# Moving the upper partitions' eighth rows of the last w_o piece to the lower 64 partitions

## The chip, the cores and the metric

The kernel runs on one core of one Trainium2 chip. The metric is the device time of one execution in microseconds (us), as the median of several runs. A profiled execution gives a trace beside it; its times count from the span's start.

## What is computed

One decode step (one row x of 576 numbers) through two branches, mixed by a gate:

```python
g = sigmoid((x * gate_w).sum())
a = attention(x @ wq, last 4096 keys and values of 16 kv heads, 32 query heads) @ wo
b = gelu(x @ w1 + b1) @ w2 + b2
return g * a + (1 - g) * b
```

w_o is 4096 x 576 and w2 is 4608 x 576, all inputs in bf16. Nothing is reused between outputs: each weight and each cached key or value is read once, 53.62 MB in all.

## The kernel before

All large loads are issued by SyncE (SP), one after the other, in the order in which the code stands: keys, wq, w1 and values, then w_o (line 617), then w2 (line 627), and at last the store of the result (line 702). Each lands in SBUF in a tile of a pool: `w_pool` has three buffers (tag "w", for wq, w1 and w_o), `kv_pool` six (tag "kv", for keys, values and w2). The whole kernel is scheduled by hand, so each engine runs its instructions in the order written.

**The loads of w_o.** Head groups of eight heads (OJ = 8, NOG = 4): in group o, partition p holds the rows o·1024 + 8p + j, j = 0 to 7, of w_o, next to each other. Line 617 loads two groups with one transfer, 128 partitions x 2 x 9,216 bytes (2304 KB); `wo_t[0]` holds groups 0 and 1, `wo_t[1]` groups 2 and 3. This text calls the two transfers wo0 and wo1.

**The loads of w2.** Four groups of 9 rows per partition. Groups 0, 1 and 2 (w2_0, w2_1, w2_2 here) are one transfer of 1296 KB each; group 3 comes in three pieces of 864, 288 and 144 KB (w2_3a, b, c).

**Completion semaphores of the transfers.** The program gives SP's transfers eight semaphores in turn (DMAHW0 to DMAHW7). Before a transfer is issued, SP waits until the transfer that had the same semaphore before, the eighth before it, has landed. SP handles its instructions strictly in order, so while one transfer waits, those behind it aren't issued. Before the change the last ones stand so in SP's list (row number, line, shape in elements, what SP waits for):

```
39 L102 v_t      64x8192     [waits DMAHW2]
40 L617 wo_t (wo0)   128x2x4608  [waits DMAHW3]
41 L617 wo_t (wo1)   128x2x4608  [waits DMAHW4]
42 L627 w2_t (w2_0)  128x5184    [waits DMAHW5, PE]
43 L627 w2_t (w2_1)  128x5184    [waits DMAHW6, PE]
44 L627 w2_t (w2_2)  128x5184    [waits DMAHW7, PE]
45 L627 w2_t (w2_3a) 128x3456    [waits DMAHW0, PE]
46 L627 w2_t (w2_3b) 128x1152    [waits DMAHW1]
47 L627 w2_t (w2_3c) 128x576     [waits DMAHW2]
48 L702 out      4x144       [waits DMAHW3, DVE]
```

**The end of the kernel.** After the last attention values, DVE scales the head outputs (`ot`, line 631), eight small matmuls lay them out by partition (`ow_ps`, line 637), and DVE picks each partition's own head by a mask (`ow_m`, line 639) and a sum (`ow`, line 647): `ow[p, j, o]` is the factor for row j of partition p in group o. Then, at line 669, `blocks` of four columns are multiplied on TensorE into the accumulator `part`: first w_o's eight blocks, each with two matmuls of 288 columns per row, 64 matmuls; then the blocks of w2_0, w2_1, w2_2 with 18 matmuls each. DVE adds the bias and scales (`part_s`, line 677). At line 688 eight matmuls collect part_s and 36 matmuls multiply w2's last group into `y_ps`; DVE copies `y` (line 701) and SP stores it (line 702).

Of the kernel before, what the change touches and what calls it, by code (L numbers as in the profile page):

```python
# [8 lines left out]
FP32 = mybir.dt.float32  # L9
BF16 = mybir.dt.bfloat16  # L10
ACT = mybir.ActivationFunctionType
ALU = mybir.AluOpType
# [4 lines left out]
def kernel(  # L17
# [15 lines left out]
    nc = tc.nc  # L33

    P = 128
    D = 576
    Hq, Hkv, Dh = 32, 16, 128
# [41 lines left out]
    const = ctx.enter_context(tc.tile_pool(name="const", bufs=1))  # L79
# [15 lines left out]
    OJ = 8  # L95
    NOG = Hq // OJ
    wo_view = A_wo.rearrange("(o p j) n -> p o (j n)", p=P, j=OJ)
# [13 lines left out]
    def load_v(m):  # L111
        return load_kv(A_v_cache, m, "v_t")

    WMAX = 36 * 256

    def load_flat(src, lo, n, name):
        t = w_pool.tile([P, WMAX], BF16, name=name, tag="w")
        nc.sync.dma_start(out=t[:, 0:n], in_=src[:, lo : lo + n])
        return t
# [17 lines left out]
    for i in range(2):  # L137
# [16 lines left out]
        out=row_f[:], in_=ident_f[:, 0 : 32 * (NQ - 1) + 1 : 32], axis=AX.X, op=ALU.add  # L154
# [4 lines left out]
        out=dup[:].rearrange("k (i e) -> k i e", e=2),  # L159
        in_=ident[0 : P // 2, 0 : P // 2].rearrange("k (i e) -> k i e", e=1).to_broadcast(  # L160
            [P // 2, P // 2, 2]
        ),
    )
    par = const.tile([P, 2], FP32, name="par")
    for o in range(2):
        nc.vector.tensor_reduce(
            out=par[:, o : o + 1],
            in_=ident_f[:].rearrange("p (i o) -> p o i", o=2)[:, o, :],
# [7 lines left out]
        out=turn[:].rearrange("p j (h q) -> p j h q", h=OJ),  # L176
        in_=ident[:].rearrange("p (o q j) -> p j o q", o=1, j=OJ).to_broadcast(
            [P, OJ, OJ, P // OJ]
        ),
# [4 lines left out]
        out=m_r[:], in_=ident_f[:].rearrange("p (s r) -> p r s", r=R), axis=AX.X, op=ALU.add  # L184
# [5 lines left out]
        out=row_e[:], in_=ident_f[:].rearrange("p (a e q) -> p e a q", e=2, q=2), axis=AX.XY,  # L190
# [3 lines left out]
        out=row_e[:], in0=row_e[:], scalar1=-MASK, scalar2=MASK, op0=ALU.mult, op1=ALU.add  # L194
    )
    mask = const.tile([P, BC * P], BF16, name="mask")
    for e in range(2):
        nc.vector.tensor_copy(
            out=mask[:, e::2], in_=row_e[:, e : e + 1].to_broadcast([P, BC * P // 2])
# [4 lines left out]
        out=m_c[:], in_=ident_f[:].rearrange("p (t c r) -> p c t r", c=BC, r=R), axis=AX.XY,  # L204
        op=ALU.add,
    )
    m_hl = const.tile([P, OJ], FP32, name="m_hl")
    nc.vector.tensor_reduce(
        out=m_hl[:], in_=ident_f[:].rearrange("p (h q) -> p h q", h=OJ), axis=AX.X, op=ALU.add
# [10 lines left out]
    for dst, src in ((sel, ident), (sel_f, ident_f)):  # L220
        nc.vector.tensor_copy(
            out=dst[:].rearrange("p l (o h) -> p l o h", o=2),
            in_=src[:].rearrange("p (h l x) -> p l x h", h=2, l=2)[:, :, 0:2, :],
# [149 lines left out]
    for dst, src, s in (  # L373
# [10 lines left out]
        out=junk[:], in0=x_row[:], in1=gw_row[:], scale=1.0, scalar=0.0,  # L384
        op0=ALU.mult, op1=ALU.add, accum_out=s0[:],
# [10 lines left out]
        out=omg[:], in0=g_t[:], scalar1=-1.0, scalar2=1.0, op0=ALU.mult, op1=ALU.add  # L396
# [7 lines left out]
    for b in range(NM * NQ):  # L404
        m, t = b // NQ, b % NQ
# [22 lines left out]
    for m in range(HB // 2):  # L428
        lo = R * (NGR - 1) + RP * m
        nc.vector.tensor_copy(  # L430
            out=qz[:, m :: HB // 2, lo : lo + RP],
            in_=qT[:, :, m, :].rearrange("p i b -> p b i"),
# [114 lines left out]
    for h in range(NU):  # L547
# [4 lines left out]
        if h == 1:  # L552

            for o in range(2):
                nc.sync.dma_start(
                    out=b1_r[o : o + 32 * (NQ - 1) + 1 : 32],
                    in_=B_b1.rearrange("(o t k n) -> o t k n", o=2, t=NQ, k=2)[o],
# [56 lines left out]
    wo_t = []  # L614
    for i in range(NOG // 2):
        t = w_pool.tile([P, WMAX], BF16, name="wo_t", tag="w")
        nc.sync.dma_start(  # L617
            out=t[:, 0 : 2 * OJ * D].rearrange("p (o n) -> p o n", o=2),
            in_=wo_view[:, 2 * i : 2 * i + 2, :],
        )  # L620
        wo_t.append(t)
    w2_t = []
    for g in range(NG):
        t = kv_pool.tile([P, NCK * Dh], BF16, name="w2_t", tag="kv")
# [7 lines left out]
        out=ot[:], in0=o_sb[:], scalar=g_t[:, 0:1], in1=r_sums[:], op0=ALU.mult, op1=ALU.mult  # L632
    )

    ow_ps = ps_m.tile([P, OJ, Hq], FP32, name="ow_ps", tag="m")
    for j in range(OJ):
# [3 lines left out]
        out=ow_m[:],  # L640
        in0=ow_ps[:].rearrange("p j (o h) -> p (j o) h", h=OJ),
        in1=m_hl[:].rearrange("p (o h) -> p o h", o=1).to_broadcast([P, OJ * NOG, OJ]),
        op=ALU.mult,
    )
    ow = const.tile([P, OJ, NOG], BF16, name="ow")
    with nc.allow_low_precision("one of the eight summands is not zero"):
        nc.vector.tensor_reduce(  # L647
            out=ow[:].rearrange("p j o -> p (j o)"), in_=ow_m[:], axis=AX.X, op=ALU.add
        )


    part = part_box[0]
    y_ps = ps_s.tile([P, DQ], FP32, name="y_ps", tag="s")
    nc.vector.memset(y_ps[:], 0.0)
    blocks = [
        [(ow[:, i, o : o + 1], wo_t[o // 2], (o % 2) * OJ + i) for i in range(j, j + NQ)]
        for o in range(NOG)
        for j in range(0, OJ, NQ)
    ]
    for g in range(NG - 1):  # L660
        for j in range(0, RJ, NQ):
            blocks.append(
                [(gt[:, i, g : g + 1], w2_t[g], i) for i in range(j, min(j + NQ, RJ))]
            )
    last = {t: max(n for n, four in enumerate(blocks) if t < len(four)) for t in range(NQ)}
    for n, four in enumerate(blocks):
# [11 lines left out]
        out=part_s[:], in0=b2_r[:].rearrange("p (k n) -> p k n", k=2), scalar=omg[:, 0:1],  # L678
        in1=part[:, :, 0:DB], op0=ALU.mult, op1=ALU.add,
# [15 lines left out]
    for j in range(RJ):  # L695
# [7 lines left out]
        out=out.rearrange("a b (t n) -> (a b t) n", t=NQ), in_=y[0 : 32 * (NQ - 1) + 1 : 32, :]  # L703
# [31 lines left out]
```

## Time and profile before

| what | value |
|---|---|
| median of 3 runs | 135.0 us (134.98 to 135.0) |
| the profiled execution's own time | 136.33 us |
| span in its trace, first to last instruction | 134.3 us |
| read from HBM | 53.62 MB, 399 GB/s over the span |
| SP's DMA queue | 94.5% of the 16 DMA engines' span |
| TensorE matmul busy | 90.8 us (68%) |
| VectorE busy | 60.2 us (45%) |
| ScalarE busy | 48.6 us (36%) |
| mean granted TensorE clock | 0.853 |

How to read it: the span is the time that the trace covers; the execution's own time has some 2 us around it, and this execution took 1.3 us more than the median of the runs. "SPq" is SyncE's sequencer, which issues transfers. A line of the timeline gives start, duration, engine, source line, operation, tile written <- tiles read, shape and count, and in brackets the idle time before it and what ended it. The profile writes `w_t` for w1 and w2 and `wo_t` for w_o.

### The profile page before, as it was taken

The page shows a single profiled execution, that of the slowest core. Times are in us where ns is not written, and L with a number is a line of the kernel's source. Part 1 is how long each engine was busy: PE and PEld are TensorE (multiplying, and loading weights), DVE is VectorE, ACT ScalarE, POOL GpSimd, SP SyncE. Part 2 cuts the span into 40 slices and gives each one's busy share as a digit, 9 for nine tenths or more (in the row PEclk, how much of TensorE's full clock was granted, in tenths as well). Part 3 has the DMA queues.
Part 4 walks back from the last instruction along what each step waited for, and adds up shares of the span by engine and source line. Part 5 has one row for each costly group of instructions (what it writes and reads, how often), then busy time and mean ns, then how long its engine had stood idle before and what let it go on. Part 6 is the DMA issues. An engine that isn't in the chain of part 4 may idle for free.

```text
span 134.3 us, 2686 instructions
## 1 busy us (share of the span) xinstructions
PE 90.8 (68%) x1127; PEld 58.1 (43%) x1127; DVE 60.2 (45%) x165; ACT 48.6 (36%) x91; POOL 5.2 (4%) x11
## 2 busy tenths in 40 slices
PE   0007985298296899397898769969969365585370
PEld 0007941265264665254565447636644141342140
DVE  4934642135127665135486544476665544400020
ACT  3003660058136787136558411557751200000000
POOL 8700000000000000000000000000000000000000
PEclk9999999959959999959999995589999965558655
DMA  3999999999999999999999999999999999999930
GB/s 78 435 431 412 406 440 444 424 448 417 426 424 429 429 449 419 412 434 424 432 420 420 434 444 420 439 424 429 434 424 429 403 436 423 422 440 423 408 128 0
DMA packets 4809, 53.79 MB, mean 400 GB/s; under 512 B 819, under 2 KB 958, under 8 KB 1342
## 3 DMA queue, kind: packets, MB, share of 16 engines
q1 hardware_dynamic: 4792, 53.62, 94.5%
q8 instruction: 9, 0.15, 0.4%
q14 instruction: 2, 0.02, 0.0%
q10 hardware_dynamic: 6, 0.00, 0.0%
HBM read 53.62 MB, written 0.00 MB: 399 GB/s over the span
## 4 chain that ended last, share of the span: by engine, by line
DMA 74%; PE 15%; DVE 6%; SPq 1%; issue 1%; DVEq 0%
DMA w_t<-in_B_w_dram 48%; DMA v_t<-in_A_v_cache_dram 17%; DMA wq_t<-in_A_wq_dram 9%; PE tp L233 6%; PE acc L340 2%; DVE kT L242 2%; PE hT L479 2%; PE s_ps L264 2%; PE y_ps L688 1%; PE part L669 1%; SPq L102 1%; DVE a_s L356 1%; DVE ez L318 1%; DVE part_s L677 1%; DVE h_r L470 1%
## 5 line engine op out<-in xcount | busy, mean ns | idle before, releaser
L244 ACT CAST kT<-tp 128x512 bf16<-128x512 f32 x80 | 44.1, 587 | 42.6 <-PE tp L233 42.3
L242 DVE CAST kT<-tp 128x512 bf16<-128x512 f32 x48 | 33.0, 690 | 36.9 <-PE tp L233 32.6
L233 PE MATMUL tp<-ident,k_t 128*128 128x128 bf16 x512 | 46.3, 242 | 4.5 <-DMA k_t<-in_A_k_cache_dram 2.9
L233 PEld LDWEIGHTS <-k_t 128*128 128x128 bf16 x512 | 35.9, 109 | 17.8 <-issue 17.1
L340 PE MATMUL acc<-v_t,ez 128*32 128x512 bf16 x128 | 13.1, 453 | 2.4 <-DVE a_s L356 2.1
L264 PE MATMUL s_ps<-kT,qz 128*32 128x512 bf16 x128 | 13.7, 423 | 0.3 <-DVE qz L430 0.3
L669 PE MATMUL part<-w_t,gt 128*1 128x288 bf16 x54 | 4.0, 384 | 4.3 <-DMA w_t<-in_B_w_dram 4.3
L452 PE MATMUL h_ps<-w_t,x 128*32 128x288 bf16 x72 | 3.1, 310 | 4.8 <-DMA w_t<-in_B_w_dram 4.8
L677 DVE SCALAR_TENSOR_TENSOR part_s<-b_r,omg,part 128x576 f32<-128x576 bf16 x1 | 0.8, 812 | 12.2 <-PE part L669 12.2
L371 PE MATMUL x_ps<-x,dup 64*128 64x9 bf16 x1 | 0.2, 163 | 8.9 <-DMA x<-in_A_x_dram 8.9
L340 PEld LDWEIGHTS <-ez 128*32 128x32 bf16 x128 | 3.7, 102 | 5.7 <-issue 3.5
L264 PEld LDWEIGHTS <-qz 128*32 128x32 bf16 x128 | 3.3, 94 | 3.9 <-issue 1.0
L669 PEld LDWEIGHTS <-gt 128*1 128x1 bf16 x54 | 2.0, 99 | 6.3 <-issue 5.1
L669 PE MATMUL part<-wo_t,ow 128*1 128x288 bf16 x64 | 4.0, 443 | 1.0 <-DVE ow L647 1.0
L452 PEld LDWEIGHTS <-x 128*32 128x32 bf16 x72 | 2.1, 99 | 5.5 <-issue 5.3
L356 DVE SCALAR_TENSOR_TENSOR a_s<-acc,m_c,a_s 128x128 f32<-128x128 f32 x12 | 4.2, 351 | 0.4
L305 ACT ACTIVATE pr<-ms,nb 128x512 bf16<-128x512 f32 x4 | 2.9, 722 | 4.1 <-DVE nb L302 4.1
L318 DVE COPY ez<-pT 128x64 bf16<-128x64 bf16 x32 | 3.6, 183 | 1.5 <-PE pT L313 1.3
L363 PE MATMUL o_ps<-m_r,a_s 128*128 128x8 f32 x8 | 1.7, 290 | 3.2 <-DVE a_s L356 3.2
L479 PE MATMUL hT<-sel_f,h_r 128*64 128x4 f32 x36 | 2.7, 265 | 1.3 <-DVE h_r L470 1.3
L363 PEld LDWEIGHTS o_ps<-m_r,a_s 128*128 128x128 f32 x8 | 1.4, 219 | 4.9 <-DVE a_s L356 2.5
L290 PE MATMUL mT<-ident_f,mx 128*1 128x128 f32 x4 | 1.1, 270 | 3.2 <-DVE mx L283 3.2
(82 smaller groups left out, 52.5 us busy)
## 6 DMA issues: line engine op xcount, KB each, us to landing
k_t<-in_A_k_cache_dram SPq DMA_DIRECT2D x16, 1024.0 KB, 18.5
v_t<-in_A_v_cache_dram SPq DMA_DIRECT2D x16, 1024.0 KB, 17.6
wq_t<-in_A_wq_dram SPq DMA_DIRECT2D x2, 2304.0 KB, 14.2
w_t<-in_B_w_dram SPq DMA_DIRECT2D x2, 2304.0 KB, 21.6
wo_t<-in_A_wo_dram SPq DMA_DIRECT2D x2, 2304.0 KB
w_t<-in_B_w_dram SPq DMA_DIRECT2D x3, 1296.0 KB, 23.8
w_t<-in_B_w_dram SPq DMA_DIRECT2D x1, 864.0 KB
w_t<-in_B_w_dram SPq DMA_DIRECT2D x1, 576.0 KB, 18.3
```

The source lines that it names most:

```text
L233: nc.tensor.matmul(tp[:, c * P : (c + 1) * P], lhsT=k_tiles[h // 2][:, (h % 2) * NCH + i * BC + c, :], rhs=ident[:], start=True, stop=True,)
L242: nc.vector.tensor_copy(out=dst, in_=tp[:])
L244: nc.scalar.copy(out=dst, in_=tp[:])
L264: nc.tensor.matmul(s_tiles[b][32 * t : 32 * (t + 1), :], lhsT=qz[:, h // 2, lo : lo + 32], rhs=kT[h][:, i * BC * P : (i + 1) * BC * P], st ...
L305: nc.scalar.activation(out=pr[:], in_=ms[:], func=ACT.Exp, bias=nb[:, 0:1], scale=SCALE, accum_out=sums[:, b : b + 1],)
L318: nc.vector.tensor_copy(out=ez[:, b % 2, m, NQ * s : NQ * (s + 1), :, RP * m : RP * (m + 1)], in_=pT[:].rearrange("p c (t s r) -> p t c s ...
L340: nc.tensor.matmul(acc[b][32 * ct : 32 * ct + 4 * R, :, :], lhsT=ez[:, b % 2, ul // 2, n, :, :].rearrange("p c r -> p (c r)"), rhs=v_tiles ...
L356: nc.vector.scalar_tensor_tensor(out=a_s[:], in0=acc[b][:, c, :], scalar=m_c[:, c : c + 1], in1=a_s[:], op0=ALU.mult, op1=ALU.add,)
L363: nc.tensor.matmul(o_ps[:], lhsT=a_s[:], rhs=m_r[:], start=True, stop=True)
L452: nc.tensor.matmul(h_box[0][32 * t : 32 * (t + 1), k, 0:FB], lhsT=x2[:, m, :], rhs=w[:, off : off + FB], start=(m == 0), stop=(m == NM - 1),)
L479: nc.tensor.matmul(box[0][64 * e : 64 * (e + 1), j, :], lhsT=rows[:, j : j + RJ * 63 + 1 : RJ], rhs=sel_f[:, e, :], start=True, stop=True,)
L669: nc.tensor.matmul(part[32 * t : 32 * t + 1, k, 0:DB], lhsT=col, rhs=w[:, i * D + k * DB : i * D + (k + 1) * DB], start=(n == 0), stop=(n ...
```

## The change

`wo_t[0]` is loaded as before. For `wo_t[1]`, group 2 is a transfer of its own for all 128 partitions (called wo1a below, 1152 KB), and of group 3 only the first seven rows are loaded for all 128 partitions (wo1b, 1008 KB). The eighth rows, 1,152 bytes for each partition, come by 16 transfers (called t1 to t16) of eight rows each: t1, t3, ... bring the rows of the partitions r, r+8, ..., r+56 to the same partitions; t2, t4, ... bring the rows of the partitions 64+r, 64+r+8, ... to the partitions r, r+8, ..., into 576 columns more on the lower 64 partitions. For this WMAX grows from 36·256 to 39·256 elements.

The factors have to follow the rows: DVE makes the factors `ow_x` of the upper partitions' eighth rows on the lower 64 partitions, with a masked sum over 64 x 4 elements and a copy of 64 x 1. Row j = 7 of group 3 is multiplied on 64 partitions, and one block of one column (two matmuls) is added behind w_o's blocks.

```diff
-    WMAX = 36 * 256
+    WMAX = 39 * 256
...
     wo_t = []
     for i in range(NOG // 2):
         t = w_pool.tile([P, WMAX], BF16, name="wo_t", tag="w")
-        nc.sync.dma_start(
-            out=t[:, 0 : 2 * OJ * D].rearrange("p (o n) -> p o n", o=2),
-            in_=wo_view[:, 2 * i : 2 * i + 2, :],
-        )
+        rows = t[:, 0 : 2 * OJ * D].rearrange("p (o n) -> p o n", o=2)
+        if i == 0:
+            nc.sync.dma_start(out=rows, in_=wo_view[:, 0:2, :])
+        else:
+            LO, J = P // 2, OJ - 1
+            nc.sync.dma_start(out=rows[:, 0, :], in_=wo_view[:, 2, :])
+            nc.sync.dma_start(out=rows[:, 1, 0 : J * D], in_=wo_view[:, 3, 0 : J * D])
+            for r in range(8):
+                for a, col in ((0, (2 * OJ - 1) * D), (LO, 2 * OJ * D)):
+                    nc.sync.dma_start(
+                        out=t[r:LO:8, col : col + D],
+                        in_=wo_view[a + r : a + LO : 8, 3, J * D : OJ * D],
+                    )
         wo_t.append(t)
...
+    ow_xm = const.tile([LO, OJ // 2], FP32, name="ow_xm")
+    ow_xf = const.tile([LO, 1], FP32, name="ow_xf")
+    nc.vector.tensor_tensor_reduce(
+        out=ow_xm[:], in0=ow_ps[0:LO, J, Hq - OJ // 2 : Hq], in1=m_hl[0:LO, 0 : OJ // 2],
+        scale=1.0, scalar=0.0, op0=ALU.mult, op1=ALU.add, accum_out=ow_xf[:],
+    )
+    ow_x = const.tile([LO, 1], BF16, name="ow_x")
+    nc.vector.tensor_copy(out=ow_x[:], in_=ow_xf[:])
...
+    blocks[-1][-1] = (ow[0:LO, J, NOG - 1 : NOG], wo_t[1][0:LO, :], 2 * OJ - 1)
+    blocks.append([(ow_x[:], wo_t[1][0:LO, :], 2 * OJ)])
```

In SP's list the 17 more transfers stand between wo0 and w2, and they take the semaphores in turn like all others (t3 to t7 and t10 to t15 left out):

```
40 L619 wo_t (wo0)   128x2x4608  [waits DMAHW3]
41 L625 wo_t (wo1a)  128x4608    [waits DMAHW4]
42 L626 wo_t (wo1b)  128x4032    [waits DMAHW5]
43 L629 wo_t (t1)    8x576       [waits DMAHW6]
44 L629 wo_t (t2)    8x576       [waits DMAHW7]
...
50 L629 wo_t (t8)    8x576       [waits DMAHW5]
51 L629 wo_t (t9)    8x576       [waits DMAHW6]
...
58 L629 wo_t (t16)   8x576       [waits DMAHW5]
59 L639 w2_t (w2_0)  128x5184    [waits DMAHW6, PE]
60 L639 w2_t (w2_1)  128x5184    [waits DMAHW7, PE]
61 L639 w2_t (w2_2)  128x5184    [waits DMAHW0, PE]
62 L639 w2_t (w2_3a) 128x3456    [waits DMAHW1, PE]
```

## The prediction

> **What bounds the kernel now.** First the page's slices of the span (the busy share of the DMA engines in tenths, and what they moved) and its chain of work by engine:
>
> ```profile
> DMA  3999999999999999999999999999999999999930
> GB/s 78 435 431 412 406 440 444 424 448 417 426 424 429 429 449 419 412 434 424 432 420 420 434 444 420 439 424 429 434 424 429 403 436 423 422 440 423 408 128 0
> DMA 74%; PE 15%; DVE 6%; SPq 1%; issue 1%; DVEq 0%
> ```
>
> The DMA engines are full from the second slice to the last but two. Every microsecond in which they have nothing to move is lost: no later slice has room to make it up. Second, the timeline of the last 19 us, TensorE and then SP's queue (86 us to the end):
>
> ```profile
> 116.28 4.01 PE L669 MATMUL part<-wo_t,ow 128*1 128x288 bf16 x64 [0.97 <-DVE ow L647]
> 120.77 1.55 PE L669 MATMUL part<-w_t,gt 128*1 128x288 bf16 x18 [0.48 <-DMA w_t<-in_B_w_dram]
> 123.86 0.90 PE L669 MATMUL part<-w_t,gt 128*1 128x288 bf16 x18 [1.54 <-DMA w_t<-in_B_w_dram]
> 126.99 1.60 PE L669 MATMUL part<-w_t,gt 128*1 128x288 bf16 x18 [2.24 <-DMA w_t<-in_B_w_dram]
> ```
>
> ```profile
> 93.52 1.11 SPq L617 DMA_DIRECT2D wo_t<-in_A_wo_dram  x2
> 96.37 11.82 SPq L627 DMA_DIRECT2D w_t<-in_B_w_dram  x6
> 131.61 0.58 SPq L702 DMA_DIRECT2D out_dram<-y  x1
> ```
>
> TensorE waits for each w2 group. The chain of waits puts 0.04 us between a landing and the matmuls, so w2_0, w2_1 and w2_2 landed at 120.73, 123.82 and 126.95: **3.1 us for 1296 KB**. SP issued them at 96 to 104, over 20 us ahead. That lead is what keeps the engines full, and the change touches it. The end of the chain:
>
> ```profile
> 102.27 24.68 DMA w_t<-in_B_w_dram
> 126.95 0.04 issue
> 126.99 1.61 PE part L669 x16
> ...
> 128.63 0.82 DVE part_s L677
> ...
> 129.50 1.76 PE y_ps L688 x44
> ...
> 131.28 0.31 DVE y L701
> ```
>
> From w2_2's landing to SP's store are 131.61 - 126.95 = 4.66 us, whenever it lands. The last w2 pieces land at most 3.1 us behind w2_2 (1296 KB in all), and the matmuls on them run until 131.25, 4.3 us behind it, so they hide there.
>
> Third, SP's waits from 86 us on (who, for whom: total, times, longest):
>
> ```profile
> SPq L702 <- DMA wo_t<-in_A_wo_dram: 4.0, 1, 4.0
> SPq L627 <- DMA v_t<-in_A_v_cache_dram: 2.6, 3, 2.1
> ```
>
> Neither transfer reads the tile that it waits for: these are the turns of the eight semaphores, on the chip. The store waited for wo0, the eighth before it, and w2_3c for a value load, until its issue at 106.71.
>
> **The change, step by step.**
>
> 1. *When wo1b has landed.* wo1 landed 3.1 us before w2_0: 120.73 - 3.1 = 117.63. wo1a and wo1b follow in the same queue without a gap, with 144 KB less: 144/1296 of 3.1 = 0.34 us. So wo1b lands at 117.3. Loads before it are as they were.
>
> 2. *Which small transfers are issued by then.* By the list of the changed program t1 to t5 wait for value loads; the last of them landed before wo0, so their issue is hidden. t6 waits for wo0, which ends the 4.0 us wait of SP at about 112.2 (117.63 less 2304/1296 of 3.1). t7 waits for wo1a, about 115. **t8 waits for wo1b**, the last big load in the queue. Behind t8 on SP stand t9 to t16 and all of w2. When t8 may go, at 117.3, the DMA engines hold nothing but tiny rests. The lead of 20 us is gone.
>
> 3. *SP's time from t8 to w2_0.* Nine issues (t8 to t16); t9 to t15 wait for small transfers issued well before, t16 for t8, some 5 us old by then. The nearest row for one issue is the other load of short rows, b1's two transfers of four rows of 1,152 bytes (SP's timeline, 3.7 to 9.9 us):
>
> ```profile
> 3.32 0.45 SPq L118 DMA_DIRECT2D wq_t<-in_A_wq_dram  x1
> 3.81 4.17 SPq L102 DMA_DIRECT2D k_t<-in_A_k_cache_dram  x4
> 8.67 1.21 SPq L555 DMA_DIRECT2D b_r<-in_B_b_dram  x2
> ```
>
> (1.21 + 0.05 gap)/2 = 0.63 us; 9 x 0.63 = 5.7 us. Bounds: the closest two issues are 0.49 us apart (3.32 and 3.81), which makes 4.4 us; the widest of the first four, in the chain of waits, are 0.68 us apart (2.00 and 2.68), 6.1 us. w2_0 is issued at 117.3 + 5.7 = 123.0.
>
> 4. *Starting up an empty queue.* Before, this cost nothing, since w2_0 stood in the queue. The one other start from empty is the first key load: issued at 0.73, landed when SP issued its eighth successor,
>
> ```profile
> 6.20 0.48 SPq L102 DMA_DIRECT2D k_t<-in_A_k_cache_dram  x1
> ```
>
> so 5.45 us for 1024 KB, of which 1024/1296 of 3.1 = 2.45 us are moving: 3.0 us of start, the upper bound. The lower bound is the store, with 1 KB: issued at 131.61, its packets began 1.2 us later, landed at 133.2: 1.6 us. In the key load's packet records the first packet began 1.4 us after the issue; the first packets took 0.7 us more than the steady 0.61; landing comes 0.3 us after the last packet. I take 1.4 + 0.7 + 0.3 = 2.4 us, without the stragglers.
>
> The Trainium skill (DMA: Bandwidth & Descriptors, section Latency and other measured facts) gives about 0.6 us to the first byte of a transfer issued from SyncE or ScalarE. The trace has 1.2 and 1.4 us from the issue's start, 0.6 to 0.8 us from its end. With 0.6 in place of 1.4 the estimate would come out 0.8 us lower, 142.2 us.
>
> 5. *Moving w2_0 to w2_2:* 3 x 3.1 = 9.3 us.
>
> 6. *An instruction fetch.* The page counts nine packets on the instruction queue. One, at 120.25 in the packet records, took 0.88 us of an engine. After the change it may fall into the empty time or onto one engine in the middle of w2: 0 to 0.9 us, I take 0.2.
>
> 7. *Compute edits.* Three small DVE instructions (nearest rows: 0.42 for 128x256, 0.17 for 128x8, at most 1.0 us together) stand behind `ow`; their result is needed when t16 has landed, about 124. Two matmuls more, 4.01/64 = 0.06 us each, 0.13 us. Both hide before w2_0's landing at 128.7. Without that cover they would cost at most 1.1 us. The tail stays 4.66 us: TensorE's granted clock was 0.50 there, the lowest in the trace. At a higher clock 18 matmuls took 0.90 instead of 1.60 us, so it can only gain, by up to 0.7 us in this step.
>
> **Sum.** w2_2 lands at 123.0 + 2.4 + 9.3 + 0.2 = 134.9, against 126.95: +7.95 us, say +8.0. This is a difference within one span (134.3 to 142.3), and for the profiled execution 136.33 to 144.3. I apply it to the median of 135.0: **143.0 us**.
>
> Bounds: 117.3 + 4.4 + 1.6 + 9.3 = 132.6 (+5.7), and 117.3 + 6.1 + 3.0 + 9.3 + 0.9 = 136.6 (+9.7): **140.6 to 144.7**.
>
> **Rivals.**
>
> *A, the other side: the queue never runs dry.* It decides at one point: if w2_0 is issued before wo1b lands at 117.3. Then the DMA engines of the upper partitions move eight rows of 1,152 bytes less each (0.34 us by step 1); if these end last, every later landing comes that much earlier, and the time is 134.7. For it: the lead was 20 us, and 17 more issues at 0.63 us (10.7 us) fit into it. Against it: t8's wait stands in the program, and SP did wait in this way for 4.0 us. Chance 4%.
>
> *B, it doesn't run dry, and the lower half is overloaded.* The trace doesn't say which DMA engines take eight-row transfers. If the same eight take all 16, each gets 16 rows where it had 8. 1,152-byte packets start 0.047 us apart in w2_3c: 16 x 0.047 - 0.34 = +0.41 us, with the completions about +0.5, 135.5. The Trainium skill (DMA: Bandwidth & Descriptors, section Why a DMA increments its semaphore by 16 and not by 1) states this: a transfer of eight rows runs on the eight lowest-numbered engines. By that rule all 16 fall on one half; no trace here shows it yet. Chance 2%.
>
> *C, the queue runs dry, but small issues are cheap.* On ScalarE's queue two one-row issues began 0.25 us apart (1.28 and 1.53). Nine at 0.25 are 2.3 us instead of 5.7: 139.6. Against it: SP's own four-row issues took 0.6. Chance 5%.
>
> *D, each small transfer waits for the one before to land,* at 1.6 us (the store): 9 x 1.6 = 14.4 us, 8.7 more: 151.7. Against it: the semaphores differ for eight in a row. Chance 3%.
>
> **Chances.** The forecast 86%, A 4%, B 2%, C 5%, D 3%. The range leaves out A to D, 14%, and a little of the forecast's own spread. About 0.2% (0.3 us) is what a measurement of this kernel tells from no change: faster 4% (A), within 0.2% 1%, slower 95%.
>
> **What would show it.** In the changed profile: a hole of 6 to 8 us in the slices' DMA line from about 117 us on; SP waiting for wo_t ahead of t8, then nine issues some 0.6 us apart; the first w2 issue near 123 instead of 96; w2 landings 3.1 us apart from about 128.7; 4.7 us from w2_2's landing to the store. It is wrong if a w2 issue stands before 117, if the hole is under 4 us, or if the issues of t9 to t16 are split by waits.

## The result, and the profile after

The changed kernel takes **145.03 us** (median of 4 runs, 144.66 to 145.21) against 134.99 for the kernel before on the same chip: a ratio of 1.0733, 95% interval 1.0699 to 1.0766, 10.0 us slower. The forecast was 143.0, with a range up to 144.7: the direction and the empty queue were right, the size 2 us short, and the time lies above the range.

The slices of the changed kernel's page (3.6 us each) show the hole that was looked for: three slices at 3, 1 and 4 tenths, together 2.2 slices or 7.9 us without work. In the chain by engine DMA has fallen from 74%, and SP's sequencer (SPq) has come in:

```profile
DMA  4999999999999999999999999999999931499930
GB/s 96 426 440 442 417 435 412 423 454 406 439 434 434 422 434 413 430 416 437 439 417 425 430 425 434 434 439 430 430 405 419 433 128 20 115 439 423 407 113 3
DMA 57%; PE 26%; DVE 6%; SPq 6%; issue 2%; DVEq 0%
```

SP's timeline from 85 us on, and, asked for 117 to 123.2 us alone, the nine issues:

```profile
96.93 25.84 SPq L629 DMA_DIRECT2D wo_t<-in_A_wo_dram  x16
122.87 3.15 SPq L639 DMA_DIRECT2D w_t<-in_B_w_dram  x6
139.72 0.58 SPq L726 DMA_DIRECT2D out_dram<-y  x1
```

```profile
117.34 5.43 SPq L629 DMA_DIRECT2D wo_t<-in_A_wo_dram  x9
```

The first w2 issue stands at 122.87. In the kernel before it stood at 96.37. SP's waits after 86 us name the reason (t6, t7 and t8 wait for wo0, wo1a and wo1b), and in their last line the wait for the store:

```profile
SPq L629 <- DMA wo_t<-in_A_wo_dram: 9.3, 3, 4.9
SPq L754 <- DMA out_dram<-y: 1.9, 1, 1.9
```

TensorE's timeline at the end:

```profile
128.25 1.60 PE L693 MATMUL part<-w_t,gt 128*1 128x288 bf16 x18 [3.35 <-DMA w_t<-in_B_w_dram]
131.99 1.60 PE L693 MATMUL part<-w_t,gt 128*1 128x288 bf16 x18 [2.15 <-DMA w_t<-in_B_w_dram]
135.09 1.60 PE L693 MATMUL part<-w_t,gt 128*1 128x288 bf16 x18 [1.50 <-DMA w_t<-in_B_w_dram]
```

w2_0, w2_1 and w2_2 landed at 128.21, 131.95 and 135.05 (0.04 us ahead of each row). Against the profile that the prediction had, the store is issued 8.1 us later (139.72 against 131.61), where 8.0 was forecast. But the span grew by 9.0 us and the median by 10.0. The kernel before is itself not always the same: of 59 executions of it beside the experiments, 12 took 135.7 to 136.1 us and the others 134.8 to 135.6. So two questions were put to the chip: is the empty queue the cause, and where do 2 us more come from?

### The profile page after: what moved, and what is told of

The parts are those of the page before. It is cut to its first block, busy times and chain, and to the rows that moved or that the text cites. A ratio compares the mean times of both kernels' runs of the same rounds, so it can differ in the third digit from the quotient of the medians.

```text
span 143.3 us, 2713 instructions
## 1 busy us (share of the span) xinstructions
PE 96.1 (67%) x1129; PEld 61.0 (43%) x1129; DVE 61.7 (43%) x168; ACT 48.9 (34%) x91; POOL 4.2 (3%) x11
## 4 chain that ended last, share of the span: by engine, by line
DMA 57%; PE 26%; DVE 6%; SPq 6%; issue 2%; DVEq 0%
DMA w_t<-in_B_w_dram 25%; DMA k_t<-in_A_k_cache_dram 17%; DMA wo_t<-in_A_wo_dram 15%; PE tp L233 12%; PE s_ps L264 4%; SPq L629 4%; PE acc L340 3%; DVE kT L242 3%; PE hT L479 2%; PE y_ps L712 1%; PE part L693 1%; PE h_ps L452 1%; DVE ms L283 1%; DVE a_s L356 1%; PE pT L313 1%
## 5 line engine op out<-in xcount | busy, mean ns | idle before, releaser
L233 PE MATMUL tp<-ident,k_t 128*128 128x128 bf16 x512 | 48.3, 249 | 4.5 <-DMA k_t<-in_A_k_cache_dram 3.0
L233 PEld LDWEIGHTS <-k_t 128*128 128x128 bf16 x512 | 37.8, 113 | 18.2 <-issue 17.3
L264 PE MATMUL s_ps<-kT,qz 128*32 128x512 bf16 x128 | 14.6, 450 | 0.3 <-DVE qz L430 0.3
L693 PE MATMUL part<-w_t,gt 128*1 128x288 bf16 x54 | 4.8, 435 | 7.0 <-DMA w_t<-in_B_w_dram 7.0
L693 PE MATMUL part<-wo_t,ow 128*1 128x288 bf16 x64 | 4.5, 430 | 2.1 <-issue 1.2
L693 PEld LDWEIGHTS <-ow 128*1 128x1 bf16 x64 | 2.1, 117 | 4.4 <-issue 1.8
L146 DVE CAST ident_f<-ident 128x128 f32<-128x128 bf16 x1 | 3.0, 3000 | 1.8 <-POOL ident masks.py:199 1.8
```

The costliest lines, as they stand in the source:

```text
L146: nc.vector.tensor_copy(out=ident_f[:], in_=ident[:])
L233: nc.tensor.matmul(tp[:, c * P : (c + 1) * P], lhsT=k_tiles[h // 2][:, (h % 2) * NCH + i * BC + c, :], rhs=ident[:], start=True, stop=True,)
L264: nc.tensor.matmul(s_tiles[b][32 * t : 32 * (t + 1), :], lhsT=qz[:, h // 2, lo : lo + 32], rhs=kT[h][:, i * BC * P : (i + 1) * BC * P], st ...
L693: nc.tensor.matmul(part[32 * t : 32 * t + 1, k, 0:DB], lhsT=col, rhs=w[:, i * D + k * DB : i * D + (k + 1) * DB], start=(n == 0), stop=(n ...
```

## The experiments

Twelve kernels ran. Two theories and their rivals: **the empty queue** (the order in SP's list and the turn of eight semaphores let the DMA engines run out of work) against **the small transfers themselves** (each one, or each of the 128 short rows, costs the DMA engines a fixed time). Differences below are against the runs of the kernel before on the same chip (135.1 to 135.3).

### The kernel before, profiled again

> The kernel before, unchanged. The changed kernel took 10.0 us more by the medians, but its profiled execution put the store only 8.1 us later than the one of before, and its span 9.0 us. Theory 1: the profiled execution of before was 1.3 us above the median of its kernel (136.33 against 135.0), so another profile of it has a span near 133.0 us, with w2_2 landing and the store issued about 1.3 us earlier (125.7 and 130.3). Theory 2: that execution was typical from its first to its last instruction and the rest lies outside the span; then the span is 134.3 again.

Measured: 135.07 us, ratio 0.9995 (0.9967 to 1.0022), a span of 133.1 us. Theory 1 held for the span and for the store's issue (130.37): the first profile was of an execution 1.3 us above its kernel's median. It missed where the time lies: w2_2 was to land 1.3 us earlier, at 125.7, and came at 126.58. TensorE's timeline at its end, the store's issue and SP's last wait:

```profile
126.63 0.90 PE L669 MATMUL part<-w_t,gt 128*1 128x288 bf16 x18 [1.22 <-DMA w_t<-in_B_w_dram]
128.43 0.42 PE L688 MATMUL y_ps<-part_s,row_f 128*1 128x144 f32 x8 [0.91 <-DVE part_s L677]
```

```profile
130.37 0.59 SPq L702 DMA_DIRECT2D out_dram<-y  x1
```

```profile
SPq L730 <- DMA out_dram<-y: 1.0, 1, 1.0
```

w2_2 lands at 126.58 (first profile: 126.95, where one of the 16 DMA engines is 0.40 us behind the next), and the 18 matmuls on it take 0.90 us in place of 1.60, so that the store is issued 3.79 us behind the landing in place of 4.66. The granted clock goes with that difference. Here are the windows of the first profile of this kernel, of the second (both 125 to 131) and then of the changed one (132 to 140); the number after the engines is the clock:

```profile
125.00:128.00 3.00, 1.01 (x17) 0.60 (x17) 0.00 (x0) 0.00 (x0) 0.00 (x0) 0.59 0.97 401
128.00:131.00 3.00, 2.10 (x50) 1.27 (x45) 0.81 (x1) 0.00 (x0) 0.00 (x0) 0.50 0.27 97
```

```profile
125.00:128.00 3.00, 1.30 (x22) 0.62 (x19) 0.44 (x1) 0.00 (x0) 0.00 (x0) 1.00 0.94 387
128.00:131.00 3.00, 1.33 (x44) 0.81 (x44) 0.68 (x2) 0.00 (x0) 0.00 (x0) 0.96 0.22 80
```

```profile
132.00:136.00 4.00, 2.50 (x34) 1.25 (x34) 0.00 (x0) 0.00 (x0) 0.00 (x0) 0.50 0.98 416
136.00:140.00 4.00, 2.43 (x50) 1.37 (x45) 1.12 (x2) 0.00 (x0) 0.00 (x0) 0.50 0.31 115
```

Against the second profile the changed kernel's 10.2 us of span are three pieces: w2_2 lands 8.47 us later (135.05 - 126.58), the stretch from there to the store's issue grows by 0.88 (4.67 - 3.79), and from the store's issue to the end by 0.85 (143.3 - 139.72 = 3.58 against 133.1 - 130.37 = 2.73).

### Fewer and more small transfers

The same 128 rows, in the same place of SP's list, cut into another number of transfers:

```diff
-            for r in range(8):
-                for a, col in ((0, (2 * OJ - 1) * D), (LO, 2 * OJ * D)):
+            for a, col, cuts in ((0, (2 * OJ - 1) * D, LOWER), (LO, 2 * OJ * D, UPPER)):
+                for r, step in cuts:
                     nc.sync.dma_start(
-                        out=t[r:LO:8, col : col + D],
-                        in_=wo_view[a + r : a + LO : 8, 3, J * D : OJ * D],
+                        out=t[r:LO:step, col : col + D],
+                        in_=wo_view[a + r : a + LO : step, 3, J * D : OJ * D],
                     )
```

> The changed kernel with the same 128 short rows in 6 transfers (four of 16 rows, two of 32) in place of 16. Theory dry queue: with six, w2_0 is the eighth transfer behind wo1a, so it waits only until wo1a has landed (114.5), while wo1b still has 2.7 us to move; the queue doesn't run dry, and the time is that of before, 135.0 within 0.5 us. Rival per transfer: each small transfer costs the DMA engines a fixed part of the 10.0 us (0.63 us each); then 6 cost 3.8 us, 138.8 us. Rival packets: the 128 packets of 1,152 bytes cost it, however they are grouped; then 145.0.

> As the one with six, but seven transfers (six of 16 rows, one of 32). Theory dry queue: w2_0 now waits for wo1b, the last big transfer in the queue. SP issues it at 117.35, with no small issue between, and the queue is empty for the start-up time alone: the changed kernel's 2.2 us from the issue to the steady stream. Against the changed kernel the nine issues of 0.61 us (5.5 us) are gone: 145.0 - 5.5 = 139.5, a step of about 4 us for one more transfer than six. Rival per transfer: 135.0 + 7 x 0.63 = 139.4, but only 0.6 more than with six. Rival packets: 145.0.

> As the one with seven, but eight transfers of 16 rows. Theory dry queue: t8 waits for wo1b, and one issue of 0.61 us stands ahead of w2_0: 140.1, 0.6 above seven. Rival per transfer: 135.0 + 8 x 0.63 = 140.0, 1.2 above six. Rival packets: 145.0.

> The changed kernel with the short rows in 32 transfers of four rows. Theory dry queue: 16 issues more of 0.61 us stand between the landing of wo1b and w2_0's issue, which moves from 122.9 to 132.6, and w2_2's landing by as much: 9.7 us on top, a span of 153.0. Rival rows: no more than the changed kernel, 143.3. The other rival, that completions 0.19 us apart set the pace, gives 16 x 0.19 = 3.0 us on top, 146.3.

| small transfers | time, us | ratio, 95% interval | w2_0 issued | w2_0 landed | w2_2 landed |
|---|---|---|---|---|---|
| 6 | 137.83 | 1.0216 (1.0163 to 1.0268) | 114.41 | 121.35 | 127.52 |
| 7 | 139.97 | 1.0360 (1.0317 to 1.0402) | 117.08 | 122.48 | 128.84 |
| 8 | 141.06 | 1.0442 (1.0423 to 1.0462) | 117.47 | 123.06 | 130.59 |
| 16 (the change) | 145.03 | 1.0733 (1.0699 to 1.0766) | 122.87 | 128.21 | 135.05 |
| 32 | 152.74, one run | - | 131.07 | 136.42 | 142.66 |

(With eight, one DMA engine lags 1.3 us in w2_2; the other 15 had landed it by 129.29.)

With seven, w2_0 is issued as soon as wo1b has landed (117.02), and with each transfer more it moves by one issue: the times rise by 0.5 us per transfer from 8 to 16 ((145.03 - 141.06)/8) and from 16 to 32. The rival of the rows would have no slope at all. The rival per transfer isn't decided by these times: the step from six to seven was to be 4 us by the theory and 0.6 by the rival, and measured 2.1; and seven, eight and 16 transfers at 0.63 us each would give 139.4, 140.0 and 145.1. Against it stand here w2_0's issue, which waits for wo1b, and the hole in the DMA lines; the next experiments decide. The 32 were forecast 2 us too late, mostly because 25 issues took 13.93 us, 0.56 each, not 0.61 (SP, 116 to 134 us):

```profile
117.04 13.93 SPq L631 DMA_DIRECT2D wo_t<-in_A_wo_dram  x25
```

The DMA line of the pages with 7 and with 32 small transfers shows the hole open, in slices of 3.4 and 3.8 us:

```profile
DMA  3999999999999999999999999999999997699920
```

```profile
DMA  4999999999999999999999999999996000099950
```

Six was a miss: 137.83, where the theory said 135.0 (the rival per transfer, with 138.8, was closer). Its trace shows no free ride: w2_0's issue waits for wo1a's landing (SP's waits):

```profile
SPq L641 <- DMA wo_t<-in_A_wo_dram: 4.5, 2, 2.2
```

At 114.41 this was before wo1b's last landing. By the landing events, wo1b's 16 landings lie between 115.03 and 116.97, so some DMA engines are 2 us ahead of others. But an engine that ran dry isn't what made w2 late: the queue stays busy around that time. Two windows of one microsecond; the last two numbers are the busy share of the DMA engines, which can come out a little above 1, and the GB/s:

```profile
115.25:116.25 1.00, 0.36 (x4) 0.00 (x0) 0.55 (x2) 0.00 (x0) 0.00 (x0) 0.50 0.93 318
116.25:117.25 1.00, 0.02 (x1) 0.02 (x1) 0.85 (x3) 0.00 (x0) 0.00 (x0) 0.50 1.11 348
```

The engines are busy, and move less. The last landings of the six small transfers follow wo1b's 0.2 to 0.3 us apart, from 117.28 to 118.22, and w2_0's last landing comes 3.1 us behind that, at 121.35, at the full pace. So the six took 1.25 us where the same rows had taken 0.34: 0.9 us lost, and as far as the landings tell, to the small transfers themselves. That is a price per transfer, 0.2 us and not 0.63. Another 1.5 us lie behind the store's issue (131.35 to 135.56, 4.2 us in place of 2.7): SP's wait for the store accounts for 1.0 of them (2.0 in place of 1.0; for this see the last experiments), and the rest stays open.

### The small transfers, but not in front of w2

> The changed kernel with the 128 short rows in two transfers of 64 rows. With six transfers the first w2 issue came at 114.4, too late for the DMA engines that had got ahead of the slowest one, and the time was 137.8. Theory dry queue: with two, w2_0 waits for a value load that lands at about 101.8 and is issued some 15 us ahead of need; no engine runs dry; w2_2 lands as before (126.6 within 0.4) and the time is 135.0 to 135.5. Rival per row of 1,152 bytes: the cost is in the 128 short packets; then the 2.7 us of six transfers stay. A smaller question: the four kernels with short transfers that were looked at have an 8 KB fetch on the second instruction queue 1.15 us behind the store's issue, and one of the store's four engines lands 0.9 to 1.0 us behind the others; the two profiles of before have it 3.8 us behind, after the end. If it hangs on the length of SP's program, three transfers more may be too few for it, and the store takes 2.7 us to the end as before.

Measured: 137.11 us, ratio 1.0129 (1.0099 to 1.0159): 1.8 us, neither 0 to 0.5 nor the full 2.7. w2_0 is issued at 101.52, so nothing is dry, yet w2_2 lands at 127.79, 1.2 us late, and the store takes 3.5 us. This too says that the late w2 of the kernel with six, which landed at 127.52, needs no dry queue.

In the next one all 16 eight-row transfers stay, but go early and into a tile of their own:

```diff
+    w8 = const.tile([P // 2, 2 * D], BF16, name="w8")
+    eighth = [(r, a) for r in range(8) for a in range(2)]
+
+    def load_eighth():
+        if eighth:
+            r, a = eighth.pop(0)
+            nc.sync.dma_start(
+                out=w8[r : P // 2 : 8, a * D : (a + 1) * D],
+                in_=wo_view[a * P // 2 + r : (a + 1) * P // 2 : 8, 3, (OJ - 1) * D : OJ * D],
+            )
...
+        if h >= HB:
+            load_eighth()
+            load_eighth()
```

> All 16 eight-row transfers of the change, on SP's queue, but into a tile of their own and issued two by two between the key and value loads of the first two thirds, with megabytes queued behind them; SP's list ends wo0, wo1a, wo1b, w2 as without them. Theory dry queue: the 10 us go. What is left is the balance of the halves (the eight lower engines get 16 rows of 1,152 bytes in 53 ns each and lose 0.34 us: +0.5 us on the lower half, -0.34 on the upper) and, if it hangs on SP's longer program, the late store (+0.9): 135.0 to 136.5 us. Rival per transfer: an eight-row transfer costs its engines much more than its packets (its completions arrive 0.19 us apart in the changed profile): 16 x 0.19 - 0.34 = 2.7 us, 137.7 us or more. Rival of the change's own idea: the upper half ends last and w2_2 lands 0.34 us earlier: 134.7.

Measured: 136.54 us, ratio 1.0080 (1.0054 to 1.0107). **The same 16 transfers, the same rows and the same computation cost 1.2 us here, and 10.0 at the place where the change has them.** That decides for the empty queue: 8.8 us of the 10.0 are the place. (The tile is another one too, but in SP's list of the changed kernel the 16 wait for no tile, only for the turns of the semaphores.) The rival that completions 0.19 us apart set the pace (137.7 or more) falls for this place, and so does the change's idea: with a full queue the shift of rows to the lower half gains nothing (135.3 before, 134.7 hoped for). The page's DMA line has no hole:

```profile
DMA  3999999999999999999999999999999999999930
```

> The changed kernel with the 16 eight-row transfers issued by GpSimd, where they stand in; SP's list has only wo1 in two parts. Theory dry queue: SP's list doesn't wait for them, w2 is issued some 20 us ahead, and w2_2 lands within 0.6 us of before; the store has no late engine, since SP's program is as short as before: 134.7 to 135.7 us. Rival per transfer or per row: 137 us or more, as for six transfers and above.

```diff
-                    nc.sync.dma_start(
+                    nc.gpsimd.dma_start(
```

Measured: 137.70 us, ratio 1.0161 (1.0134 to 1.0189). SP's list no longer waits for the small transfers and 7.6 of the 10.0 us are gone, but 2.4 us were not expected to stay, and the time lies where the rival had it (137 or more). The last experiments put some 0.8 of them down to the late store, which this kernel's trace has too (one of its four landings 0.85 us behind the others). For the rest there is no trace that could be compared. So it stays open what an eight-row transfer costs on GpSimd's queue; the empty queue is decided by the early transfers on SP's own.

### What is left without the empty queue

Against the kernel before, the first of the next two has one transfer of 128 rows, the second has two of 64 in its place:

```diff
+            nc.sync.dma_start(out=rows[:, 0, :], in_=wo_view[:, 2, :])
+            nc.sync.dma_start(out=rows[:, 1, 0 : J * D], in_=wo_view[:, 3, 0 : J * D])
+            nc.sync.dma_start(out=rows[:, 1, J * D :], in_=wo_view[:, 3, J * D :])
```

> The kernel before with wo1 in three transfers, group 2, group 3's rows 0 to 6 and group 3's eighth rows, all 128 partitions each and each row on its own partition; the computation is as before. It takes the idea out of the two-transfer kernel (137.1) and keeps the short packets. Theory own place: what was left there, 1.2 us on w2_2 and 0.8 us behind the store's issue, comes from the move to the lower partitions and the work added for it; this kernel takes the time of before, 135.3 within 0.3. Rival short packets: 1,152-byte packets at this place cost the 1.2 us wherever they go; then 136.4. Theory late store: the fetch 1.15 us behind the store's issue hangs on the instructions added on TensorE and VectorE, so here it is absent and the store takes 2.7 us to the end.

```diff
-            nc.sync.dma_start(out=rows[:, 1, J * D :], in_=wo_view[:, 3, J * D :])
+            for lo in (0, P // 2):
+                nc.sync.dma_start(
+                    out=rows[lo : lo + P // 2, 1, J * D :],
+                    in_=wo_view[lo : lo + P // 2, 3, J * D :],
+                )
```

> As the last one, but the eighth rows in two transfers of 64 rows, lower and upper partitions, each on its own partitions. Against the two-transfer kernel (137.1) only the place of the upper rows differs, and the added computation is gone. Theory place: w2_2 lands as before within 0.3 us, 135.3 us in all. Rival transfers of 64 partitions: two 64-row transfers bunch on half of SBUF one after the other and cost the 1.2 us by themselves, 136.5.

Measured: one 128-row transfer 134.91 us, ratio 0.9972 (0.9954 to 0.9991), w2_2 at 126.58; two 64-row transfers 135.74, ratio 1.0043 (1.0021 to 1.0065), w2_2 at 127.21. So short packets cost nothing (the rival falls); two transfers of 64 partitions in place of one of 128 cost 0.8 us, more than the theory of the place said and less than its rival; and the move to the lower half with its computation makes up the rest of the two-transfer kernel's loss (1.8 us there, 0.6 here: 1.2 us), of which 0.8 are the next finding and 0.4 stay open. The 128-row split is the fastest version tried; at 0.3% it is hardly more than what can be told from no change, and a kernel that only adds two matmuls (below) came out at 0.9979. It is no proven gain.

The last two add to the kernel before VectorE's instructions alone, as the change has them, with the result not used; and TensorE's block alone, with factors of zero:

> The kernel before with nothing but the change's three VectorE instructions added (their result isn't used). Theory late store by VectorE's program: the 8 KB fetch comes 1.15 us behind the store's issue, one of the store's engines lands about 0.9 us late, and it takes 3.5 us from the store's issue to the end, 135.0 + 0.8. If the fetch isn't VectorE's: 2.7 us and 135.0 to 135.3 as before.

> The kernel before with nothing but one more block of two matmuls on 64 partitions behind w_o's blocks, with a column of zeros for the factors. Theory late store by TensorE's program: the 8 KB fetch comes 1.15 us behind the store's issue, one engine of the store lands 0.9 us late, 3.5 us from the store's issue to the end, 135.8. If the fetch isn't TensorE's: 2.7 us, 135.0 to 135.3. If neither this one nor the VectorE one shows it, the added transfers do it.

```diff
+    zcol = const.tile([P // 2, 1], BF16, name="zcol")
+    nc.gpsimd.memset(zcol[:], 0.0)
...
+    blocks.append([(zcol[:], wo_t[1][0 : P // 2, :], 2 * OJ - 1)])
```

Measured: VectorE's three instructions alone 135.93 us, ratio 1.0058 (1.0038 to 1.0079), a span of 134.2; TensorE's block alone 135.12, ratio 0.9979 (0.9956 to 1.0002), a span of 133.1. With VectorE's instructions the last landing and the store's issue stay within 0.2 us of where they were; what grows is SP's wait for the store:

```profile
SPq L740 <- DMA out_dram<-y: 1.9, 1, 1.9
```

and in the store's window (131.0 to 134.2 us, DMA queues: packets, MB, share) there is a fetch of instructions beside the store's eight packets, which the same window of the kernel before doesn't have:

```profile
q14 instruction: 1, 0.01, 1.0%
q1 hardware_dynamic: 8, 0.00, 0.2%
```

By the packet records it is 8 KB, 1.14 us behind the store's issue, and one of the store's four landings comes 0.9 us behind the others. All nine traced kernels with VectorE's three instructions have it, and none of the five profiles without them has. That it delays the store on a DMA engine that both use fits this, but the records don't name engines; why three instructions bring the fetch to that point is not shown either.

## Why the prediction fell short, and what of it held

| step | forecast | measured |
|---|---|---|
| 1, wo1b lands | 117.3 | 117.33 |
| 2, t8 waits for it, w2 behind t8 | yes | yes (the waits, 9.3 us) |
| 3, nine issues | 5.7 us | 5.53 (117.34 to 122.87) |
| 4, start-up of the empty queue | 2.4 us | 2.24 (122.87 to 128.21, less 3.1) |
| 5, three w2 groups | 9.3 us | 9.3 without step 6 |
| 6, a fetch on one engine | 0.2 us | 0.64 |
| w2_2 lands | 134.9 | 135.05 |
| 7, compute edits | 0 | 0.85 us behind the store's issue |
| from w2_2's landing to the store | 4.66 us, "can only gain" | 4.67, but 3.79 in the kernel before |
| difference to the median | +8.0 us | +10.0 us |

**Steps 1 to 6 held within 0.2 us at their end.** The start-up that had to be bounded from two distant rows (1.6 to 3.0) was 2.24 here, 2.30 with seven, 2.49 with eight and 2.25 with 32 small transfers. The Trainium skill's 0.6 us to the first byte (DMA: Bandwidth & Descriptors, section Latency and other measured facts), in place of the row's 1.4, would have made this term 1.6: the row was right. In part the small error is luck: steps 3 and 4 came out 0.3 us shorter and step 6 0.4 us longer. And the fetch of step 6 is another one than the prediction had in view. The 16 KB at 120.25 in the first profile came at 119.9 here, into the empty time. The packet records have an 8 KB fetch at 128.94, and one of 16 engines then lands w2_1 0.64 us behind the next (131.95 against 131.31) and keeps that lag in w2_2; that the fetch made the lag is read from the times, since the records don't name engines.

**The step that failed is the last one of the sum: "I apply it to the median of 135.0".** A difference from one profiled execution was added to a median that this execution missed by 1.3 us. The note that it took 136.33 us stood in the table; what the extra time was made of was not asked. It was mostly the tail: at clock 0.50 the first profile took 4.66 us from w2_2's landing to the store, the second 3.79, and its landing was 0.37 us earlier. "It can only gain" was true of that execution, but the base had gained already, and the changed kernel stayed at 4.67. Together 1.25 us. The prediction took the 4.66 us as fixed, "whenever it lands"; the stretch goes with the clock, which was 0.50 there in one execution of the kernel before and 1.00 in the other.

In the records of the granted clock, 0.50 and 1.00 alternate in stretches of 3.41 us or multiples of it: 1.00 from 122.14 to 125.55 in the first profile, from 123.93 to 130.76 in the second, from 122.72 to 126.13 in the changed kernel. In the first profile the clock fell at 125.55, with waits of 1.54 and 2.24 us for w2 before and around it; in the changed kernel it fell at 126.13, inside a wait of 3.35 us, and stayed at 0.50 through two more of 2.15 and 1.50. In the second profile TensorE worked from 119.8 to 125.4 nearly without a break. The wait alone doesn't decide: the kernel with VectorE's instructions alone waited 2.24 us too and ran the next matmuls at the full clock:

```profile
126.79 0.90 PE L679 MATMUL part<-w_t,gt 128*1 128x288 bf16 x18 [2.24 <-DMA w_t<-in_B_w_dram]
```

The Trainium skill (TensorE: Matmul & The Clock Gate, Part 1: The HAM clock gate) states that half the clock is the idle state, entered after an idle window of about 3.4 us, and that sustained work releases it. The length of the stretches agrees; but in the first profile the clock fell with no wait longer than 2.24 us. No run changed the clock alone, so its part is read from the traces, not shown.

**The second miss is step 7.** The edits' work is hidden, as said: TensorE has done the last added matmul at 124.9, and w2_0 lands at 128.2. But their price of "at most 1.1 us without cover" was looked for in the work; the 0.8 us came at the store, from the instructions' being there at all, and the kernel with VectorE's instructions alone shows it. Either miss alone would have left the time inside the range (143.0 + 1.25, or 143.0 + 0.85); the range had no term for either.

Rival A didn't come, and wouldn't have been a gain: the kernel with the early transfers takes 136.5 with a queue that never runs dry. Rival B's 0.5 us is about what that kernel's median keeps beyond the store's 0.8, but in its trace w2_2 lands 1.1 us late (127.65 against 126.58), twice B's price. That eight-row transfers run on eight DMA engines is borne out in number: each has eight landings in the trace, and the four-row ones have four; which engines they are, the records don't say. C and D fall: issues took 0.61 us and ran back to back.

## What to carry to other kernels

Count the transfers, not only the bytes, that stand between a deep queue and the next big load: with eight completion semaphores in turn, seven small transfers behind the last big load use up the whole lead, and from then on each one more costs its issue time, about half a microsecond, on the path. A small load belongs where megabytes are queued behind it, or into one transfer over all 128 partitions. And before a difference is put on a median, check that the profiled execution is a typical one, or take the second profile first.

## What the runs showed of the hardware that was not expected

Three VectorE instructions whose result nobody used cost 0.8 us, with an 8 KB instruction fetch that then falls beside the store (SP's wait for the store 1.9 in place of 1.0 us). Two transfers of 64 partitions cost 0.8 us more than one of 128 with the same rows (135.74 against 134.91). And small transfers in a full queue have a price of their own: six of 16 or 32 rows landed 0.2 us apart and took 1.25 us, where one transfer with the same rows landed 0.36 us behind wo1b (117.26 against 116.90).
